# Three pieces of K and V per head instead of four blocks, and x read as one row, in a decode attention kernel that reads 282 MB

## The chip, the cores and the metric

One core of a Trainium2 chip. The metric is the device time of one execution in microseconds (us), median over several. The "span" is the profiled time from the first to the last instruction; it is usually some 1.4 us shorter than the time. PE is the matrix engine, DVE the vector engine, ACT the scalar engine, SP the engine whose queue issues the loads. A load "lands" when its completion is signalled; its "forerunner" is the load ahead of it in the queue, and its "lead" is how long before the forerunner's landing it is issued. Where a run fell in the slow state it is left out and named.

## The reference

One new token (batch 1) attends over a cache of 65,536 positions in 8 key/value heads, four query heads on each, followed by a small gated MLP. Everything is bf16.

```python
B, Sq, D = 1, 1, 512
Hq, Hkv, Sk, Dh = 32, 8, 65536, 128            # k_cache, v_cache: (1, 8, 65536, 128)
def _A_ref(x, k_cache, v_cache, wq, wo):
    q = (x @ wq) ...                           # 32 heads of 128
    k, v = repeat(k_cache, 4), repeat(v_cache, 4)
    scores = einsum("bhqd,bhkd->bhqk", q, k) * Dh ** -0.5
    p = softmax(scores)
    return einsum("bhqk,bhkd->bhqd", p, v) ... @ wo
x = A_x
h = x + _A_ref(layernorm(x), A_k_cache, A_v_cache, A_wq, A_wo)
g, u = layernorm(h) @ w_gate, layernorm(h) @ w_up      # 512 -> 1792
return h + (sigmoid(g) * u) @ w_down                   # 1792 -> 512
```

K and V are 134.2 MB each and are used once. The rest (w_q, w_o, the MLP) is 14 MB.

## The kernel before

K and V lie in SBUF in a ring of four slots, one slot for a block of 16,384 positions: 128 rows of 32 KB, 4 MiB. One queue (SP) issues every load in a fixed order; each load waits until what stood in its slot has been used. A head is four K blocks and four V blocks, alternating, with V one head behind K.

```python
order = [("wq", 0)]
order += [("K", b) for b in range(NR)]                       # NR = 4 blocks a head
for b in range(NR, NB):                                      # NB = 32
    order += [("K", b), ("V", b - NR)]
order += [("V", NB - 4), ..., ("V", NB - 1), ("wg", 0), ("wu", 0), ("wd", 0)]
...                                                          # slot_of, prev: who frees the slot
dma("act", lambda e: e.dma_start(x_col[:, :], A_x[0].rearrange("o (p k) -> (o p) k", k=4)), "x", name="x")
V_SPLIT = [(0, 3), (3, 4)]                                   # the very last V block comes in two pieces
...
    src = cache[0, h, r * BLK:(r + 1) * BLK, :].rearrange("(p t) d -> p (t d)", t=T)     # 128 rows of 32 KB
    dma("sp", lambda e, d=dst, sr=src: e.dma_start(d, sr), ..., deps, f"{k}{b}")
if ld == ("V", NB - 4):
    ...                                                      # w_o, after the first V block of the last head
```

```python
label("values", "part")
e.reg_mov(m, NR); e.reg_mov(k, 0); e.reg_mov(v, v_even)
...                                       # V0..V3: waits for the block, by branches once per block
goto("sums", "values")
pv_regs(e)                                # 14 register additions: the addresses of the round
goto("products", "sums")
section("B")                              # the eight matmuls
e.reg_alu(p, p, 2 * 512, ALU.add)
e.reg_alu(v, v, 2 * 2 * CH, ALU.add)
e.reg_alu(m, m, -1, ALU.add)
e.br_ne(m, 0, on_true="sums", on_false="sums_end")
```

After the last V piece come w_o's second part, a layernorm, w_gate and w_up, the gate, and w_down: 56 small matmuls, four at a time, whose weights are the last bytes to land.

Of the kernel before, what the change touches and what calls it, by code (L numbers as in the profile page):

```python
# [35 lines left out]
class Prog:  # L36
# [26 lines left out]
    def emit(self):  # L63
# [3 lines left out]
        needed = {d for ops in self.ops.values() for o in ops for d in o["deps"]} | set(self.at_end)  # L67
# [20 lines left out]
        for e, ops in self.ops.items():  # L88
            n = 0
            for o in ops:  # L90
                if o["dma"]:
                    k, v = o["dma"]
                    value[o["name"]] = (self.dma_sems[k]["sem"], v, k)
                elif o["to"]:
                    k = o["to"]
                    counts[k] = counts.get(k, 0) + 1
                    if o["name"]:
                        value[o["name"]] = (extra[k], counts[k], k)
                    o["inc"] = True
                elif o["name"] in needed or o.get("inc"):  # L100
                    n += o["times"]
                    value[o["name"] or id(o)] = (sems[e], n, e)
                    o["inc"] = True
# [110 lines left out]
def bass_sequential_preLN__gqa_block_cached__glu_gated_glu__decode_kernel(  # L214
# [10 lines left out]
    SLOT = T * DH  # L225
    CH = TC * DH
    NF = FF // 128
# [6 lines left out]
    with ExitStack() as es:  # L234
# [16 lines left out]
        ring = sb("ring", [128, NSLOT * SLOT], bf16)  # L251
# [9 lines left out]
        x_col = sb("x_col", [128, 4], bf16)  # L261
# [40 lines left out]
        def slot_ap(s):  # L302
            return ring[:, s * SLOT:(s + 1) * SLOT]

# [4 lines left out]
        order = [("wq", 0)]  # L309
        order += [("K", b) for b in range(NR)]  # L310
        for b in range(NR, NB):
            order += [("K", b), ("V", b - NR)]
        order += [("V", NB - 4), ("V", NB - 3), ("V", NB - 2), ("V", NB - 1), ("wg", 0), ("wu", 0), ("wd", 0)]
        slot_of, prev = {}, {}
        for i, ld in enumerate(order):
            if ld[0] == "V" and ld[1] >= NB - NR:
                slot_of[ld] = slot_of["V", ld[1] - 2]
                prev[ld] = ("V", ld[1] - 2)
            elif ld[0][0] == "w" and i:
                slot_of[ld] = 3 if ld[0] == "wd" else 1  # L320
                prev[ld] = ("K", NB - 1 if ld[0] == "wd" else NB - 2)
            else:
                slot_of[ld] = i % NSLOT
                prev[ld] = order[i - NSLOT] if i >= NSLOT else None

        def freed(ld):
            if ld is None:
                return None
            k, b = ld
            return {"wq": "q", "K": f"F{b}", "V": f"PV{b}"}[k]  # L330

        dma("act", lambda e: e.dma_start(x_col[:, :], A_x[0].rearrange("o (p k) -> (o p) k", k=4)), "x", name="x")
        V_SPLIT = [(0, 3), (3, 4)]
        W_SPLIT = {"wg": [(0, 4)], "wu": [(0, 3), (3, 4)]}
        W_AT = {"wg": 0, "wu": 4 * FF}
        for ld in order:
            k, b = ld
            s = slot_of[ld]
            dst = slot_ap(s)
            deps = [freed(prev[ld])]  # L340
            if k == "wq":
                dma("sp", lambda e, d=dst: e.dma_start(d.rearrange("p (k n) -> p k n", k=4),
                    A_wq.rearrange("(p k) n -> p k n", p=128)), f"r{s}", deps, "wq")
            elif k in ("wg", "wu"):
                w = B_w_gate if k == "wg" else B_w_up
                dst, src = dst[:, W_AT[k]:W_AT[k] + 4 * FF], w.rearrange("(p k) n -> p (k n)", p=128)
                for i, (k0, k1) in enumerate(W_SPLIT[k]):
                    dma("sp", lambda e, d=dst, w=src, a=k0 * FF, z=k1 * FF: e.dma_start(d[:, a:z], w[:, a:z]),
                        f"{k}{i}", deps if i == 0 else (), f"{k}.{i}")
            elif k == "wd":  # L350
                src = B_w_down.rearrange("(p r) n -> p r n", p=128)
                for i, (r0, r1) in enumerate(WD_SPLIT):
                    dma("sp", lambda e, d2=dst[:, r0 * D:r1 * D].rearrange("p (r n) -> p r n", n=D), sr=src[:, r0:r1, :]:
                        e.dma_start(d2, sr), f"wd{i}", deps if i == 0 else (), f"wd{i}")
            else:
                h, r = b // NR, b % NR
                cache = A_k_cache if k == "K" else A_v_cache
                src = cache[0, h, r * BLK:(r + 1) * BLK, :].rearrange("(p t) d -> p (t d)", t=T)
                if ld == ("V", NB - 1):
                    for i, (c0, c1) in enumerate(V_SPLIT):  # L360
                        d2, s2 = (ap[:, 2 * c0 * CH:2 * c1 * CH] for ap in (dst, src))
                        dma("sp", lambda e, d2=d2, s2=s2: e.dma_start(d2, s2),
                            "v0" if i else "vl", deps if i == 0 else (), f"V{b}.{i}")
                else:
                    dma("sp", lambda e, d=dst, sr=src: e.dma_start(d, sr), f"v{s}" if k == "V" else f"k{s}" if k == "K" and b >= NR else f"r{s}",
                        deps, f"{k}{b}")
            if ld == ("V", NB - 4):
                for i, (j0, nj) in enumerate(WO):
                    src = A_wo[j0 * DH:(j0 + nj) * DH, :].rearrange("(p r) n -> p (r n)", r=nj)
                    dst = ktw[:, j0 * D:(j0 + nj) * D]  # L370
                    dma("sp", lambda e, src=src, dst=dst: e.dma_start(dst, src), f"wo{i}",
                        [f"G{HKV - 1}"] if i == 0 else (), f"wo{i}")
# [44 lines left out]
        ln_stats(0, lambda e: e.tensor_copy(hT[0][:, :], x_col[:, :]), "x", 0, 0)  # L417
# [36 lines left out]
        def project_q(e):  # L454

            e.reg_mov(reg(e, 0), addr_of(xz, 8 + 7))
            e.reg_mov(reg(e, 4), addr_of(ring, slot_of[("wq", 0)] * SLOT))
# [3 lines left out]
            with e.Fori(0, HKV):  # L461
                for kt in range(4):
                    mm_at(e, ps(1, 0, 512, 0, 8), at_reg(xz, reg(e, kt), [[4 * 16, 128], [1, 8]]),
                          at_reg(ring, reg(e, 4 + kt), [[NSLOT * SLOT, 128], [1, 512]]), False, 32)
# [36 lines left out]
        def dve_block(b):  # L501
            s = slot_of[("K", b)]
            for c in range(NC):
                n = b * NC + c
                at = s * SLOT + (2 * (c % NR) + c // NR) * CH
                src = ring[:, at:at + CH].bitcast(fp32)
                dst = ktw[:, (n % NKT) * CH:(n % NKT + 1) * CH].bitcast(fp32)
                deps = [f"K{b}"] if c == 0 else []
                if b % NR or b == 0:
                    deps.append(f"S{b - 1}.{c}" if b else None)  # L510
                op("dve", lambda e, d=dst, sr=src: e.transpose(d, sr), deps, f"T{b}.{c}", to="T")  # L511
            op("dve", lambda e: e.memset(scr[:, b:b + 1], 0.0), (), f"F{b}")
# [49 lines left out]
        def transposed(h):  # L562

            for b in range(NR * h, NR * h + NR):
                op("dve", lambda e, b=b: e.transpose(PT_sb[:, (b % 4) * 512:(b % 4 + 1) * 512],  # L565
                                                     P_sb[:, (b % 4) * 512:(b % 4 + 1) * 512]),
                   [f"E{b}", f"oxq{h - 1}" if h else None], f"PT{b}", to="PT" if b % NR == NR - 1 else None)
# [7 lines left out]
        def pv_regs(e):  # L575
            for half in range(NC // NR):
                for tq in range(4):
                    i = 8 * half + tq
                    if i:
                        e.reg_alu(reg(e, i), R["p"], 2 * (128 * tq + half), ALU.add)  # L580
                        e.reg_alu(reg(e, i + 4), R["v"], 2 * (half * TC + 4 * tq) * 128, ALU.add)

        def pv(b):
            h, r = b // NR, b % NR
            if r == NR - 1:
                P.part["pe"] = ("VL", b)
                op("pe", lambda e: None, [f"V{b}" if b < NB - 1 else f"V{b}.1"])
            P.part["pe"] = ("B", b)
            for half in range(NC // NR):
                for tq in range(4):  # L590
                    i = half * 8 + tq
# [3 lines left out]
                        at_reg(ring, reg(e, i + 4) if i else R["v"], [[NSLOT * SLOT, 128], [1, 512]]), False, 32, 32 * tq),  # L595
                       (), f"PV{b}" if half and tq == 3 else None, times=NR)

        def head_out(h):
            op("act", lambda e: e.activation(po_sb[:, :], ps(PO, 0, 512), AF.Copy, scale=rl[:, :]),  # L599
               [f"PV{NR * h + NR - 1}", f"rl{h}"], f"po{h}", to="po")  # L600
            for t in range(4):
                op("pe", lambda e, t=t: e.matmul(ps(OX, 0, 4), lhsT=po_sb[:, t * 128:(t + 1) * 128],  # L602
                                                 rhs=sel_bf[:, 8 * t:8 * t + 8:2], start=(t == 0), stop=(t == 3)),
                   [f"po{h}"] if t == 0 else (), f"ox{h}" if t == 3 else f"oxq{h}" if t == 2 else None,
                   to="Q" if t == 2 else None)
# [30 lines left out]
        def project7():  # L636
            regroup(0)
            waits = ["O3.0", "wo0"]
            def rows(e):
                out = ps(YB, 0, D, 0, 1)  # L640
                e.matmul(out, lhsT=O3[:, 0:1], rhs=ktw[:, 0:D], start=True, stop=False, skip_group_check=True)
                ra, ro, rb, rp, left = (reg(e, i) for i in range(5))
# [26 lines left out]
        def pe_flow(e, section):  # L669
# [7 lines left out]
            i, w, p, v, m, k = (R.setdefault(n, e.alloc_register(f"r_{n}")) for n in "iwpvmk")  # L677
            w0, p0 = addr_of(ktw, W0 + NC - 1 + 127), addr_of(PT_sb, 31 * 4)
            v_even, v_odd = (addr_of(ring, slot_of[("V", b)] * SLOT) for b in (0, 1))
            e.reg_mov(i, 0)  # L680
            goto("head")
            e.reg_mov(w, w0)
            e.reg_mov(p, p0)
            goto("part")
            e.br_eq(i, HKV, on_true="last", on_false="scores")
# [9 lines left out]
            away("br_eq", w, w0 - 12, "maxima", lambda: section("X"))  # L695
            e.br_eq(i, 0, on_true="next", on_false="values")
            label("values", "part")
            e.reg_mov(m, NR)
            e.reg_mov(k, 0)
            e.reg_mov(v, v_even)  # L700

            def odd_late():
                e.reg_mov(v, v_odd)
# [168 lines left out]
```

## Time and profile before

| | before |
|---|---|
| time, median of the first 3 runs | 658.38 us (658.36 to 658.48) |
| span of the profiled run | 657.1 us |
| busy share: DMA queue / PE / DVE / ACT | 99.7% / 64% / 53% / 7% |
| x landed / projection of the query ended | 14.8 / 27.7 us |
| last V piece landed / last PV matmul ended | 641.98 / 644.21 us |
| last weights landed / the matmuls that need them start | 654.83 / 654.87 us |

The main lines of the page stand in the prediction below. A line of the timeline reads: start, duration, engine, source line, operation, destination<-sources, count, and in brackets the idle time just before and what ended it.

From the view that cuts the run into stretches, for the last 1.90 us of matrix work (columns: stretch and length, busy time and count of PE, weight loads, DVE, ACT, POOL, then PE's granted clock, the DMA share and GB/s):

```profile
653.40:655.30 1.90, 1.68 (x56) 1.26 (x56) 0.13 (x1) 0.00 (x0) 0.00 (x0) 0.50 0.50 196
```

The DMA still works in this stretch: in the kernel before, w_down's last third comes in while PE is in the earlier ones.

### The profile page before, as it was taken

Reading aid. Unit: us, or ns where it says so; the run is one execution under the profiler, and the core shown is the slowest. Engines: PE = TensorE matmul, PEld = TensorE weight load, DVE = VectorE, ACT = ScalarE, POOL = GpSimd, SP = SyncE. Lnnn points to the kernel's source line nnn. Section 1 sums busy time; section 2 is a strip of 40 time slices with the busy share of each in tenths; the row PEclk is TensorE's granted clock in tenths of the full one; section 3 lists DMA queues with packets and bytes.
Section 4 is the critical chain, followed back from the end, with each engine's and each line's share of the span. In section 5 each row is a group of like instructions: output and inputs, shape, how many; then the busy total and the mean of one; then the engine's idle time right before and its main releaser. Section 6 shows DMA issues by size and latency. Waiting matters only on the chain. (4 is left out here: it accounts for less than half of the span.)

```text
span 657.1 us, 6111 instructions
## 1 busy us (share of the span) xinstructions
PE 420.5 (64%) x2315; PEld 74.1 (11%) x1547; DVE 349.7 (53%) x439; ACT 42.9 (7%) x114; POOL 3.6 (1%) x17
## 2 busy tenths in 40 slices
PE   0688488548666585576765575764866668556746
PEld 0200011011000010010100110101100001001322
DVE  2399775547537665347555374465743575542202
ACT  1100200020000200020000200002000100002001
POOL 1000000000000000000000000000000000000000
PEclk9989689677888697776966769765888869677676
DMA  9999999999999999999999999999999999999998
GB/s 383 447 433 429 439 423 431 431 447 415 447 415 447 437 425 447 415 447 419 443 441 421 447 415 447 423 439 443 419 447 415 447 427 435 445 417 427 435 430 352
DMA packets 10802, 282.34 MB, mean 430 GB/s; under 512 B 1329, under 2 KB 1330, under 8 KB 1842
## 3 DMA queue, kind: packets, MB, share of 16 engines
q1 hardware_dynamic: 10658, 282.33, 99.7%
q10 hardware_dynamic: 144, 0.00, 0.0%
HBM read 282.33 MB, written 0.00 MB: 430 GB/s over the span
## 5 line engine op out<-in xcount | busy, mean ns | idle before, releaser
L431 PE MATMUL PS<-ktw 128*128 128x512 bf16 x1024 | 299.9, 442 | 157.4 <-DVE ktw L511 153.6
L511 DVE STREAM_TRANSPOSE ktw<-ring 128x1024 f32<-128x1024 f32 x256 | 291.6, 1205 | 128.0 <-DMA ring<-in_A_k_cache_dram 128.0
L431 PE MATMUL PS<-ring,PT_sb 128*32 x1024 | 83.9, 455 | 23.6 <-issue 13.2
L431 PEld LDWEIGHTS PS<-ktw 128*128 x256 | 27.1, 106 | 408.2 <-issue 256.8
L565 DVE STREAM_TRANSPOSE PT_sb<-P_sb 128x512 bf16<-128x512 bf16 x32 | 20.2, 684 | 54.0 <-PE PS L602 52.3
L551 ACT ACTIVATE negmax<-PS 128x1 f32<-128x1 f32 x8 | 1.4, 171 | 520.6 <-PE PS L549 520.6
L431 PEld LDWEIGHTS PS<-ring,PT_sb 128*32 x1024 | 25.8, 116 | 79.8 <-issue 74.6
L516 DVE TENSOR_REDUCE M_sb<-PS 128x1 f32<-128x512 f32 x32 | 19.9, 684 | 25.5 <-PE PS L431 25.5
L555 ACT ACTIVATE P_sb<-PS,negmax 128x512 bf16<-128x512 f32 x32 | 21.6, 686 | 0.3
L572 DVE TENSOR_REDUCE lsum<-PS 128x1 f32<-128x4 f32 x8 | 1.3, 163 | 31.2 <-PE PS L570 31.2
L542 PE MATMUL PS<-identf,gm 128*1 128x128 f32 x16 | 3.4, 301 | 16.9 <-DVE gm L540 16.9
L616 DVE TENSOR_TENSOR Lw<-O,blk_of 128x896 bf16<-128x896 bf16 (+1 forms) x2 | 1.4, 683 | 20.6 <-ACT O L606 20.6
L402 PE MATMUL PS<-st,onesf 128*128 128x2 f32 x4 | 1.2, 362 | 16.1 <-DVE st L401 16.1
L431 PE MATMUL PS<-ring,xz 128*8 x32 | 9.2, 459 | 2.3 <-issue 2.3
L599 ACT ACTIVATE po_sb<-PS,rl 128x512 bf16<-128x512 f32 x8 | 5.5, 687 | 53.2 <-PE PS L431 53.2
L431 PE MATMUL PS<-ktw,O 128*1 x26 | 7.6, 464 | 0.0
L549 PE MATMUL PS<-one_f,gmrep 1*128 1x1 f32 x16 | 4.2, 330 | 5.0 <-DVE gmrep L546 5.0
L555 ACT ACTIVATION_READ_ACCUMULATOR P_sb<-PS,negmax 128x1 f32 x32 | 6.5, 202 | 0.0
L476 DVE STREAM_TRANSPOSE qt<-qh 32x512 bf16<-32x512 bf16 x1 | 0.7, 699 | 10.6 <-ACT qh L473 10.6
L602 PE MATMUL PS<-sel_bf,po_sb 128*128 128x4 bf16 x32 | 2.0, 168 | 6.4 <-ACT po_sb L599 6.4
L417 DVE CAST hT<-x_col 128x4 f32<-128x4 bf16 x1 | 0.2, 171 | 10.6 <-DMA x_col<-in_A_x_dram 10.6
L661 DVE COPY yr<-PS 1x512 f32<-1x512 f32 x1 | 0.7, 679 | 8.3 <-PE PS L659 8.3
(82 smaller groups left out, 74.0 us busy)
## 6 DMA issues: line engine op xcount, KB each, us to landing
ring<-in_A_k_cache_dram SPq DMA_DIRECT2D x32, 4096.0 KB, 28.7
ring<-in_A_v_cache_dram SPq DMA_DIRECT2D x31, 4096.0 KB, 26.4
ring<-in_A_wq_dram SPq DMA_DIRECT2D x1, 4096.0 KB, 12.3
ktw<-in_A_wo_dram SPq DMA_DIRECT2D x1, 3584.0 KB, 12.7
ring<-in_A_v_cache_dram SPq DMA_DIRECT2D x1, 3072.0 KB, 13.2
ring<-in_B_w_gate_dram SPq DMA_DIRECT2D x1, 1792.0 KB, 19.0
ring<-in_B_w_up_dram SPq DMA_DIRECT2D x1, 1344.0 KB, 21.7
ring<-in_A_v_cache_dram SPq DMA_DIRECT2D x1, 1024.0 KB, 15.2
```

The source lines that it names most:

```text
L431: return e.add_instruction(mybir.InstMatmult(name=nc.get_next_instruction_name(), engine=mybir.EngineType.PE, ins=[rhs, lhsT], outs=[e.low ...
L511: op("dve", lambda e, d=dst, sr=src: e.transpose(d, sr), deps, f"T{b}.{c}", to="T")
L516: op("dve", lambda e, u=u: e.tensor_reduce(M_sb[:, u % 4:u % 4 + 1], ps(u % NS, 0, 512), AX.X, ALU.max), [f"S{b}.{NC - NR + k}"], f"mx{u}" ...
L542: op("pe", lambda e: e.matmul(ps(MISC, 0, 128, 0, 1), lhsT=gm[:, :], rhs=identf[:, :], start=True, stop=True), [f"gm{h}"], f"gmT{h}", to="Q")
L549: op("pe", lambda e: e.matmul(ps(MISC, 128, 129), lhsT=gmrep[0:1, :], rhs=one_f[0:1, 0:1], start=True, stop=True), [f"gmrep{h}"], f"neg{h}")
L551: op("act", lambda e: e.activation(negmax[:, k:k + 1], ps(MISC, 128, 129), AF.Copy, scale=-att_scale), [f"neg{h}"], f"negmax{h}")
L555: op("act", lambda e, b=b: e.activation(P_sb[:, (b % 4) * 512:(b % 4 + 1) * 512], ps(b % NS, 0, 512), AF.Exp, bias=negmax[:, k:k + 1], sca ...
L565: op("dve", lambda e, b=b: e.transpose(PT_sb[:, (b % 4) * 512:(b % 4 + 1) * 512], P_sb[:, (b % 4) * 512:(b % 4 + 1) * 512]), [f"E{b}", f"o ...
L572: op("dve", lambda e: e.tensor_reduce(lsum[:, :], ps(MISC, 132, 136), AX.X, ALU.add), [f"l{h}"], f"ls{h}", to="D")
L599: op("act", lambda e: e.activation(po_sb[:, :], ps(PO, 0, 512), AF.Copy, scale=rl[:, :]), [f"PV{NR * h + NR - 1}", f"rl{h}"], f"po{h}", to ...
L602: op("pe", lambda e, t=t: e.matmul(ps(OX, 0, 4), lhsT=po_sb[:, t * 128:(t + 1) * 128], rhs=sel_bf[:, 8 * t:8 * t + 8:2], start=(t == 0), s ...
L616: op("dve", lambda e: e.tensor_tensor(Lw[i][:, :].rearrange("p (j c) -> p j c", j=n), bass.AP(tensor=O2, offset=j0, ap=[[NQ, 128], [1, n], ...
```

## The change

Its intent: fewer and longer transfers, so that less is lost between them. A head's K and V come in three pieces of 48, 32 and 48 KB a row (12, 8 and 12 chunks) instead of four of 32 KB; rows of the cache are assigned to partitions by piece. The ring keeps its size, but its places now overlap between heads, so the order of loads and what frees them are written out. w_o is issued between the first two V pieces of the last head. x is read as one row of 1 KB and turned into four columns by four matmuls. On PE, the wait for a piece can now fall in the middle of a loop of ten rounds, so the round itself tests whether it has come to a wait. The diff also moves work that has nothing to do with the loads: DVE transposes a head's probabilities only after the first eight chunks of the next head, and the matmuls that turn w_o's row into columns (2.0 us at 638.08 before) come ahead of the last head's second piece.

```diff
-        x_col = sb("x_col", [128, 4], bf16)
+        x_row = sb("x_row", [1, D], bf16)
...
+    PIECES = ((0, 12), (12, 20), (20, 32))
+    AT = {"K": (0, 0, 8), "V": (12, 24, 20), "K0": (0, 12, 20), "V7": (0, 12, 20), "wq": 24, "wg": 0, "wd": 7}
...
+        dma("act", lambda e: e.dma_start(x_row[:, :], A_x[0]), "x", name="x")
+        LAST = [(20, 28), (28, 32)]
...
+            rows = cache[0, h, j0 * TC * 128:j1 * TC * 128, :].rearrange("(p t) d -> p (t d)", p=128)
...
+        for h in range(1, HKV):
+            load("K", h, 0, ["F0.1" if h == 1 else f"F{h - 1}.3"], "ka", f"K{h}.0")
+            load("V", h - 1, 0, ["F0.3" if h == 1 else f"PV{h - 2}.3:2"], "va", f"V{h - 1}.0")
+            load("V", h - 1, 1, ["F0.4" if h == 1 else f"PV{h - 2}.3"], "vb", f"V{h - 1}.1")
+            load("K", h, 1, [f"F{h}.0"], "ka", f"K{h}.1")
+            load("K", h, 2, [f"F{h}.1", f"PV{h - 1}.0:4"], "kb", f"K{h}.2")
+            load("V", h - 1, 2, [f"PV{h - 1}.0"], "vb", f"V{h - 1}.2")
+        h = HKV - 1
+        load("V", h, 0, [f"F{h}.3"], "va", f"V{h}.0")
...                                                   # w_o here, after PV{h - 1}.3
+        load("V", h, 1, (), "vm", f"V{h}.1")
+        for i, cols in enumerate(LAST):
+            load("V", h, 2, (), ("vb", "vl")[i], f"V{h}.2{('', 'b')[i]}", cols)
...
+        for k in range(4):
+            op("pe", lambda e, k=k: e.matmul(ps(0, 4 + k, 5 + k), lhsT=bass.AP(tensor=x_row, offset=k, ap=[[D, 1], [4, 128]]),
+                                             rhs=sel_bf[0:1, 0:1], start=True, stop=True, skip_group_check=True),
...
             goto("sums", "values")
             pv_regs(e)
+            def waits():
+                e.reg_alu(c, c, 8, ALU.add)
+                e.br_eq(w, w0, on_true="second", on_false="fourth")
+                ...                                   # the second piece, w_o's rows
+                label("fourth", "waits")
+                e.br_ne(i, i_last, on_true="products", on_false="last_rounds")
+                label("last_rounds", "fourth")
+                section("VL")                         # wait for the very last piece
+            away("br_eq", p, c, "waits", waits, "products")
             goto("products", "sums")
             section("B")
-            e.reg_alu(p, p, 2 * 512, ALU.add)
+            e.reg_alu(p, p, s, ALU.add)
+            e.reg_alu(s, s, step[0] ^ step[1], ALU.bitwise_xor)
             e.reg_alu(v, v, 2 * 2 * CH, ALU.add)
             e.reg_alu(m, m, -1, ALU.add)
```

## The prediction

No term of the forecast's sum is among them: the sum came to 0.73 + 0.05 = 0.78 us, and so to 657.6 us. The rate of 435.2 GB/s in it (its "ceiling", from which also the 99.5%, the 77.10 us, the 51.20 us and the 648.75 us come) was not yet shown by the trace of before, whose packets give 435.0. It stands because the packets of both traces give it: 8192 B are recorded as 309 ns (medians), and in the trace of after 49152 B as 1815, so 40960 B in 1506 ns, times 16 engines 435.2 GB/s. One nanosecond in the 1506 moves the 9.638 us by 6 ns, so the 46 ns per transfer are an estimate, and an experiment below gives about 40. The start-up "of about 2 us" is an estimate from the trace of before too, where the first packet starts 1.03 us after the first issue.

> **What bounds the kernel now.** I read the page from the transfers upward: HBM bytes and DMA share first, then whether the share ever drops, then what the end hangs on.

> ```profile
> span 657.1 us, 6111 instructions
> DMA  9999999999999999999999999999999999999998
> q1 hardware_dynamic: 10658, 282.33, 99.7%
> q10 hardware_dynamic: 144, 0.00, 0.0%
> HBM read 282.33 MB, written 0.00 MB: 430 GB/s over the span
> ```

> The DMA engines are busy in every slice, 99.7% of the span. PE is busy 64% and DVE 53%, so the compute engines have room. q10 is the read of x: 128 rows of 8 bytes each and 16 completions, 144 packets for 1 KB. The transfers view gives the lead with which loads are issued and the landing times:

> ```profile
> ring<-in_A_k_cache_dram SPq DMA_DIRECT2D x32, 4096.0 KB, 28.7
> ring<-in_A_v_cache_dram SPq DMA_DIRECT2D x31, 4096.0 KB, 26.4
> ring<-in_A_wq_dram SPq DMA_DIRECT2D x1, 4096.0 KB, 12.3
> x_col<-in_A_x_dram ACTq DMA_DIRECT2D x1, 1.0 KB, 14.0
> ```

> A 4 MiB load lands 28.7 us (median) after its issue although one takes under 10 us: two others stand ahead of it. The queue's own waits (over 19 us at the longest, for DVE to free K or PE to free V) are therefore hidden. The pace is best read from the waits of DVE for K, in the timeline of DVE; these two lines are six heads apart:

> ```profile
> 99.62 9.13 DVE L511 STREAM_TRANSPOSE ktw<-ring 128x1024 f32<-128x1024 f32 x8 [1.33 <-DMA ring<-in_A_k_cache_dram]
> ...
> 564.43 9.13 DVE L511 STREAM_TRANSPOSE ktw<-ring 128x1024 f32<-128x1024 f32 x8 [9.48 <-DMA ring<-in_A_k_cache_dram]
> ```

> (564.43 - 99.62) / 6 = 77.468 us per head of eight 4 MiB transfers: 9.684 us each, 433.1 GB/s, with no room for a bubble of even a microsecond. The landing records say the same: 9.67 to 9.71 us between any two neighbours from 12.3 us on.

> The end, from the timeline: the last V pieces, then the short MLP while its weights still come in.

> ```profile
> 640.17 2.72 PE L431 MATMUL PS<-ring,PT_sb 128*32 x24
> 643.26 0.91 PE L431 MATMUL PS<-ring,PT_sb 128*32 x8 [0.37 <-PEq L169]
> 648.72 3.15 PE L813 MATMUL PS<-ring,hc 128*1 128x448 bf16 x32 [0.25 <-DVE hc L800]
> 653.58 1.68 PE L831 MATMUL PS<-ring,hhT 128*1 128x128 bf16 x56 [0.98 <-DVE hhT L826]
> 655.96 0.33 SPq L841 DMA_DIRECT2D out_dram<-y_sb  x1
> ```

> The third w_down piece lands at 654.83 us (issued at 629.6, 25.2 us to landing), and its eight matmuls start at 654.87. PE had begun the ones before at 654.72, one group per 0.107 us, so without the wait it would have gone on at about 654.83. Transfers and the PE chain arrive together: the end moves earlier only if both do. After it come the y copies and the store, 2.2 us to the end of the span.

> [...] a packet of 32768 B is recorded as 1213 ns and one of 8192 B as 309 ns; the slope, 24576 B in 904 ns, times 16 engines is 435.0 GB/s. The kernel runs at 99.5% of that. [...] the 8-byte packets of x run from 5.4 to 14.4 us, eight per engine, about one per 1.2 us, which is one 32 KB packet of wq or K. [...]

> **The change part by part.**

> *Fewer, larger loads.* The bytes stay. At 435.2 GB/s 4 MiB take 9.638 us; they take 9.684, so a queued transfer costs 46 ns beyond its bytes: eight data packets and one completion per engine, 5 ns each. The tail confirms that this hardly depends on size: from the landing of V at 603.13 to the last weights at 654.83, 12 transfers of 0.26 to 4 MB bring 22.28 MB in 51.70 us; the bytes take 51.20; 0.50 / 12 = 42 ns. A piece of 48 KB a row still has 128 rows, so eight packets per engine, so again some 46 ns. Counts: before, 32 K + 33 V + 1 wq + 2 wo + 6 MLP = 74. After, 24 K + 25 V (the last piece cut in two) + 9 = 58. Saved: 16 x 0.046 = 0.73 us, all on the path that sets the end. Per head: six transfers instead of eight, 77.10 + 6 x 0.046 = 77.38 us.

> *x as a row.* 128 packets fewer. The first K intervals, in which they ran, are 9.70 and 9.71 us against 9.684: 0.04 to 0.05 us saved. x lands at some 6 to 7 us instead of 14.8, and four one-column matmuls (about 0.5 us) are added; from landing to ready query took 14.80 to 18.28 = 3.5 us, so PE could start at about 11, and then waits for wq at 12.3. The projection (9.4 us) ends near 22 instead of 27.7: 6 us earlier. Its worth at the end is zero, because the queue is full at that time: it only releases the third piece of K0 earlier.

> *Hand-offs.* Each load must be issued before its forerunner has landed, less a start-up of about 2 us (first issue at 0, first bytes between 1 and 2 us). The smallest lead in the old trace, w_o's issue at 598.92 against a landing at 603.13, is 4.2 us and left no visible gap. New order in a head: K0, V0, V1, K1, K2, V2 of 14.5, 14.5, 9.7, 9.7, 14.5, 14.5 us. With t = 0 at the start of K0: K2 lands at 62.9, DVE needs four transposes of 1.14 us, so the next K0 is issued at 67.7, due at 77.4: lead 9.7. K1 (free after eight chunks of K0, about 24; due 38.7) 14. K2 (four PV rounds of 0.9 us after V0 has landed at 29, about 33; due 48.4) 15. V2 (all ten rounds, 43; due 62.9) 20. The next V0 (two of the last six rounds, about 82; due 91.9) 10. At the first head, where softmax lies between, K1 of head 1: its forerunner lands at 89.7, head 0's softmax ends near 72, eight transposes to 82: about 7. w_o after the first V7 piece: PV of head 6 ends near 602, due 608: 6. All above 4.2, so no stall is expected.

> *The end.* After the last V piece (16 KB a row instead of 8) two rounds of eight matmuls remain instead of one: 0.9 us more. But the old chain did not hang on that landing (641.98, used from 643.26, when the three rounds and the branch before it were over; PV done at 644.21 = landing + 2.23). In the new kernel the four rounds on the bigger piece (lands 4.9 us earlier) are over first; then 0.25 us to start and 1.85 us for two rounds: landing + 2.1. The four fp32 column matmuls (2.0 us at 638.08, just ahead of the old last rounds) move into the idle time before. So chain and weights shift alike.

> Sum: 0.73 + 0.05 = 0.78 us; 658.38 - 0.78 = 657.6 us.

> **The rivals.**

> 1. *The start counts.* Six microseconds earlier query, so about 652. For it: PE's wait before the projection and the late x. Against: DMA 9 in the first slices, and K landing every 9.7 us all through the projection.
> 2. *The larger pieces stall the queue.* Three pieces give coarser releases, and PE now waits for V1 in the middle of a part. A lead that shrinks to nothing costs its shortfall once per head: 1 us each would give 664 or so. Against: the leads above, and compute at half load.
> 3. *Long rows are cut into more packets.* Nothing before is longer than 32768 B. If 48 KB became two packets at 5 ns each, 32 pieces with eight extra per engine cost 1.3 us, more than is saved: 658.9.
> 4. *The PE chain takes the end.* If the two rounds, or fetching their branch code, come out 0.9 us longer than counted, nothing is left of the gain, since the chain has no slack to the weights: 658.5.

> **Range and chances.** Rivals 3 and 4 put the upper end near 658.7; a somewhat larger saving per transfer, or a shorter tail, the lower at 656.8. The old bytes alone take 648.75 us at the ceiling, and start-up (2.6 us before steady flow) and end (2.3 us after the last landing, 1.3 us from span to time) stay, so even with no per-transfer cost at all it would be some 655: faster by over 2% (645.2) is shut out by the bytes. Slower by 2% (671.6) needs rival 2 on a large scale. 0.005, 0.985, 0.01.

> **What would show it right or wrong.** DMA queue: near 8450 packets (58 x 144 and the store) if 48 KB is one packet. DVE's waits for K: 77.38 us per head. x: landing below 8 us, projection from about 12.5. Last weights at about 654.05. A 7 or 8 in the DMA row, or K waits further apart than 77.5, would mean rival 2; about 12500 packets rival 3; last weights early but the end unmoved, rival 4. A first-slice gain that survives to the end would refute my claim that x is hidden.

## More of the kernel before

The "granted clock" is the share of its full speed at which PE is let run.

Before, PE's timeline at the last head's third block:

```profile
632.81 3.61 PE L431 MATMUL PS<-ring,PT_sb 128*32 x32 [6.47 <-PEq L169]
```

Thirty-two matmuls are four rounds; their first matmuls start at 632.81, 633.64, 634.49 and 635.35, so a round takes 0.85 us.

## The result, and the profile after

| | before | after |
|---|---|---|
| time, median of 6 runs each | 658.46 us (658.36 to 658.98) | 657.96 us (657.40 to 658.45) |
| ratio, with 95% interval | | 0.9991 (0.9978 to 1.0004): the same |
| span of the profiled run | 657.1 us | 657.1 us |
| last V piece landed / last PV matmul ended | 641.98 / 644.21 us | 640.91 / 644.33 us |
| last weights landed | 654.83 us | 653.75 us |

A ratio here is the mean time of one kernel's fast runs over the mean of the other's of the same rounds, so it is not quite the ratio of the medians quoted. Lines of the page after:

```profile
DMA  9999999999999999999999999999999999999997
...
q1 hardware_dynamic: 8354, 282.33, 99.5%
q10 hardware_dynamic: 2, 0.00, 0.0%
```

8354 packets are 58 transfers of 144 and two for the store: a row of 48 KB is one packet (recorded as 1815 ns; 32 KB took 1213). q10, the read of x, went from 144 packets to 2. No slice but the last shows a digit below 9; that one fell from 8 to 7, because the transfers end earlier in it. In DVE's timeline, the waits for K six heads apart:

```profile
99.30 9.13 DVE L500 STREAM_TRANSPOSE ktw<-ring 128x1024 f32<-128x1024 f32 x8 [9.94 <-DMA ring<-in_A_k_cache_dram]
...
563.49 9.13 DVE L500 STREAM_TRANSPOSE ktw<-ring 128x1024 f32<-128x1024 f32 x8 [16.25 <-DMA ring<-in_A_k_cache_dram]
```

(563.49 - 99.30) / 6 = 77.365 us per head, against 77.468 before. At the start, PE's timeline:

```profile
7.00 0.29 PE L402 MATMUL PS<-sel_bf,x_row 1*128 1x1 bf16 x4 [7.00 <-DMA x_row<-in_A_x_dram]
...
12.87 9.81 PE L419 MATMUL PS<-ring,xz 128*8 x32 [4.35 <-DMA ring<-in_A_wq_dram]
```

x is there at 7.0 instead of 14.8, and the projection now waits for w_q and is over at 22.7 instead of 27.7. So far this is the prediction. The end is not quite; PE's timeline there, and the store:

```profile
636.67 4.47 PE L419 MATMUL PS<-ring,PT_sb 128*32 x32 [3.70 <-PEq L171]
642.15 2.17 PE L419 MATMUL PS<-ring,PT_sb 128*32 x16 [1.01 <-issue]
...
653.47 1.66 PE L823 MATMUL PS<-ring,hhT 128*1 128x128 bf16 x56 [0.97 <-DVE hhT L818]
...
655.82 0.33 SPq L833 DMA_DIRECT2D out_dram<-y_sb  x1
```

The four rounds on the bigger part of the last block take 4.47 us where four took 3.61; they start at 636.67, 637.82, 638.98 and 640.09, 1.11 to 1.16 us apart. The granted clock does not explain this: it was 0.50 in both stretches. At that clock rounds written out without registers start 0.84 to 0.85 us apart (in an experiment below), just as the old ones do, so the old round was as long as its matmuls; its sequencer's work was some 0.76 us (two rounds at a clock of 1.00, from 624.2 us on in the trace of before) and lay hidden behind them. The new round is as long at either clock. These are the last two rounds of the run with the pieces alone (below), the first of them at a clock of 1.00:

```profile
642.30 0.63 PE L415 MATMUL PS<-ring,PT_sb 128*32 x8 [1.43 <-issue]
643.41 1.01 PE L415 MATMUL PS<-ring,PT_sb 128*32 x8 [0.48 <-issue]
```

Eight matmuls are over in 0.63 us, and the next eight still start 1.11 us after the first: in the new loop the sequencer sets the pace.

The store is only 0.14 us earlier than before (655.82 against 655.96). The chain of what ended last shows the same stretch step by step (start, duration, what):

```profile
640.09 1.05 PE PS L419 x6
641.14 1.01 issue
642.15 1.05 PE PS L419 x8
643.20 0.06 issue
```

The last V piece landed at 640.91, but its first round starts at 642.15: 1.24 us later, of which 1.01 us lies between two rounds in which PE's sequencer was busy with nothing that the profile names ("issue"); between the other rounds it is 0.06 to 0.11. PV ends at 644.33, 0.12 us later than before, although the piece came 1.07 us earlier. PE reaches w_down at 653.47, when the last weights are about to land (653.75, 0.28 us later), and then works through the 56 matmuls without a wait. **The end has moved from the weights to the PE chain.**

With that the end depends on the clock that PE is granted in its last two microseconds. The same kernel profiled again, and the same stretch in both (first the run above, then the second):

```profile
653.40:655.30 1.90, 1.66 (x56) 1.37 (x56) 0.13 (x2) 0.12 (x1) 0.00 (x0) 0.50 0.00 0
```

```profile
653.40:655.30 1.90, 0.95 (x56) 0.77 (x56) 0.56 (x2) 0.54 (x2) 0.00 (x0) 1.00 0.00 0
```

At a clock of 0.50 the matmuls take 1.66 us, at 1.00 they take 0.95; the spans of the two runs are 657.1 and 656.3. The DMA share is 0 in both, where it was 0.50 before. The six spans of the changed kernel (657.1, 657.0, 656.9, 656.3, 656.0, 656.0) fall into two groups 0.6 to 1.1 us apart, as this would make them; the mean granted clock of a whole run (0.774 to 0.786) does not tell the groups apart, and only profiled runs show the clock of the last stretch.

### The profile page after: what moved, and what is told of

It reads as the page before. It is cut to its first block, busy times and chain, and to the rows that moved or that the text cites. A ratio compares the mean times of both kernels' runs of the same rounds, so it can differ in the third digit from the quotient of the medians.

```text
span 657.1 us, 6298 instructions
## 1 busy us (share of the span) xinstructions
PE 441.4 (67%) x2319; PEld 70.5 (11%) x1551; DVE 350.4 (53%) x432; ACT 42.9 (7%) x114; POOL 3.6 (1%) x17
## 2 busy tenths in 40 slices
DMA packets 8356, 282.33 MB, mean 430 GB/s; under 512 B 930, under 2 KB 932, under 8 KB 1444
## 3 DMA queue, kind: packets, MB, share of 16 engines
q1 hardware_dynamic: 8354, 282.33, 99.5%
HBM read 282.33 MB, written 0.00 MB: 430 GB/s over the span
## 5 line engine op out<-in xcount | busy, mean ns | idle before, releaser
L419 PE MATMUL PS<-ktw 128*128 128x512 bf16 x1024 | 294.9, 440 | 109.9 <-DVE ktw L500 103.2
L419 PE MATMUL PS<-ring,PT_sb 128*32 x1024 | 105.4, 506 | 66.5 <-PEq L171 34.9
L419 PEld LDWEIGHTS PS<-ring,PT_sb 128*32 x1024 | 21.8, 116 | 145.3 <-issue 143.6
L507 DVE TENSOR_REDUCE M_sb<-PS 128x1 f32<-128x512 f32 x32 | 19.9, 684 | 19.5 <-PE PS L419 19.5
L535 DVE TENSOR_REDUCE gmj<-PS 1x4 f32<-1x128 f32 x8 | 2.2, 279 | 44.6 <-PE PS L533 44.6
L561 PE MATMUL PS<-L_sb,lsel 128*128 128x4 f32 x16 | 2.5, 229 | 3.8 <-DVE PT_sb L556 3.8
## 6 DMA issues: line engine op xcount, KB each, us to landing
ring<-in_A_v_cache_dram SPq DMA_DIRECT2D x9, 4096.0 KB, 30.1
ring<-in_A_k_cache_dram SPq DMA_DIRECT2D x8, 4096.0 KB, 24.7
ring<-in_A_wq_dram SPq DMA_DIRECT2D x1, 4096.0 KB, 12.2
ktw<-in_A_wo_dram SPq DMA_DIRECT2D x1, 3584.0 KB, 14.4
```

What stands on the lines that cost most here:

```text
L419: return e.add_instruction(mybir.InstMatmult(name=nc.get_next_instruction_name(), engine=mybir.EngineType.PE, ins=[rhs, lhsT], outs=[e.low ...
L507: op("dve", lambda e, u=u: e.tensor_reduce(M_sb[:, u % 4:u % 4 + 1], ps(u % NS, 0, 512), AX.X, ALU.max), [f"S{b}.{NC - NR + k}"], f"mx{u}" ...
L535: op("dve", lambda e: e.tensor_reduce(gmj[:, :], ps(MISC, 0, 128, 0, 1).rearrange("p (i a c) -> p a i c", a=4, c=NC), AX.XY, ALU.max), [f" ...
L561: op("pe", lambda e: e.matmul(ps(MISC, 132, 136), lhsT=lsel[:, :], rhs=L_sb[:, :], start=True, stop=True), [f"PT{NR * h + NR - 1}"], f"l{h ...
```

## The experiments

Three theories were set against each other.

- **A.** Fewer transfers save their fixed cost all along, the row of x next to nothing, and what arrives earlier at the end is partly lost because the new loop makes the rounds longer, so that the PE chain holds the end.
- **B.** The end is still on the transfers, and the longer rounds are harmless.
- **C.** The gain, as far as there is any, comes from the start (x).

### The changed kernel again, twice

> The changed kernel once more, beside the others on one chip. Theory A (the transfers got about 1 us shorter, but the PE chain after the last V piece got longer and now sets the end): last weights land near 653.8 us, the last w_down matmuls start well after that, and the time is 0 to 0.6 us below the kernel before. Rival B (the end hangs on the weights as it did before, and the small gain seen is scatter between chips): time 0.8 to 1.1 us below the kernel before.

> The changed kernel for comparison on this chip: spans from 655.9 to 657.1, the low ones in runs in which the clock granted at the end is high; last weights near 653.75 in all.

No edit. Measured: medians 657.99 and 657.95 us, ratios 0.9990 (0.9977 to 1.0003) and 0.9990 (0.9976 to 1.0004). With the first result these are three sets on different occasions whose means lie 0.62, 0.67 and 0.61 us below those of before. (The medians differ by 0.50, 0.58 and 0.31.) Each interval just includes 1; that all three means agree makes a gain of some 0.6 us likely, if far below 2%, but does not show it. The last weights land at 653.72 and 653.70 (653.75 in the first profile): the landing times repeat to 0.05 us. The spans (means 656.50 and 656.46, before 656.98 and 656.84) put the gain at 0.4 to 0.5 us. Why time and span differ by 0.2 us is not known.

### The pieces alone, and the row alone

```diff
# the pieces alone: the changed kernel with x as columns
-        x_row = sb("x_row", [1, D], bf16)
+        x_col = sb("x_col", [128, 4], bf16)
-        dma("act", lambda e: e.dma_start(x_row[:, :], A_x[0]), "x", name="x")
+        dma("act", lambda e: e.dma_start(x_col[:, :], A_x[0].rearrange("o (p k) -> (o p) k", k=4)), "x", name="x")
...
# the row alone: the kernel before with these lines the other way round
```

> The changed kernel with the old read of x (128 rows of 8 bytes). Theory A: w_q and all later loads land 0.05 to 0.1 us later than in the changed kernel, x lands near 14 us, the projection ends near 28 us and the third piece of K0 is still issued before the queue is empty; time within 0.15 us of the changed kernel. Rival (the start counts): 2 us or more slower than the changed kernel.

> The kernel before, with only x read as one row and turned by four matmuls. Theory A: x lands near 6.7 us instead of 14.8, the query is ready 5 us earlier, w_q and all later loads land 0.05 to 0.1 us earlier, the time falls by 0.05 to 0.15 us and no more, as the queue is full while the query is made. Rival (the start counts): 2 to 6 us faster.

PE's timeline at the projection with the pieces alone (with the row alone it starts at 12.83):

```profile
19.48 8.44 PE L415 MATMUL PS<-ring,xz 128*8 x32 [2.31 <-issue]
```

With the pieces alone the projection is 6.6 us later than in the changed kernel, yet every landing differs from it by no more than 0.05 to 0.13 us, and the last weights land at 653.85: 0.98 us earlier than before. Theory C falls. With the row alone they land at 654.41, 0.42 us earlier than before. The two parts do not add up to the 1.08 us of both, and the reason lies mostly in the one trace of before: against each of four other builds of it (the row alone, and three runs below, of which two also have a slower pace of their own) its landings fall back once by some 0.25 us between 61 and 119 us. What this slip is, isn't known. Without it the pieces alone save 0.73, the row alone 0.17 and both 0.83 us. The start of a run (w_q landed between 12.14 and 12.54 us in the profiles) also shifts everything after it, so the share of x, 0.1 to 0.2 us, can't be fixed more closely from single traces. In time, the pieces alone took 658.53 us (ratio 1.0000, 0.9986 to 1.0013).

The row alone took 661.61 us (ratio 1.0038, 1.0021 to 1.0055), which no theory had expected. The loss is not within the program as profiled: the spans average 656.80 against 656.98 before, but in five of six runs the time exceeds the span by 4.7 to 5.3 us instead of some 1.4. What happens in those three microseconds, and why with this build, stays open (its trace shows a packet of instructions just after the end, but so does that of before: 16 KB, 1.22 us, 1.3 us after the span). It says nothing against the row in the changed kernel, whose times exceed its spans by the usual amount.

### What a transfer costs: more packets, more transfers

The prediction put the whole gain on 46 ns per transfer. Two experiments on the kernel before separate packets from transfers. In the first each row of a K or V block is two runs of 16 KB (twice the data packets, the same 74 transfers); in the second each block is loaded by two transfers (twice the packets and twice the transfers).

```diff
# two runs
+                    src = src.rearrange("(a p t) d -> p a (t d)", a=2, p=128)
+                    dst = dst.rearrange("p (a x) -> p a x", a=2)
# two transfers
-                    dma("sp", lambda e, d=dst, sr=src: e.dma_start(d, sr), ...)
+                    for y in range(2):
+                        dma("sp", lambda e, d=dst, sr=src, y=y: e.dma_start(d[:, y * 4 * CH:(y + 1) * 4 * CH], sr[:, y * 4 * CH:(y + 1) * 4 * CH]), ...)
```

> The kernel before, with each row of K and V (but the last block's) made of two runs of 16 KB from two places: same bytes, same 74 transfers, 16 data packets per engine and transfer instead of 8. Which token a row holds changes for K and V alike, so the result stays. If the 46 ns per transfer belong to its packets (5 ns each): 62 x 8 x 5 = 2.5 us later. If they belong to the transfer: no change.

> The kernel before, with every K and V load cut into two transfers of half the row: 138 transfers instead of 74, packets of 16 KB as in the run with two runs a row. Either way 64 x 46 ns = 2.9 us later in the last landing; what it has over the run with two runs a row is the cost of a transfer beside its packets: about 0.4 us if packets carry the cost, all of 2.9 if the transfer does.

DVE's waits for K six heads apart, first with two runs, then with two transfers:

```profile
99.82 9.13 DVE L516 STREAM_TRANSPOSE ktw<-ring 128x1024 f32<-128x1024 f32 x8 [2.87 <-DMA ring<-in_A_k_cache_dram]
...
566.33 9.13 DVE L516 STREAM_TRANSPOSE ktw<-ring 128x1024 f32<-128x1024 f32 x8 [9.33 <-DMA ring<-in_A_k_cache_dram]
```

```profile
100.01 9.13 DVE L514 STREAM_TRANSPOSE ktw<-ring 128x1024 f32<-128x1024 f32 x8 [2.20 <-DMA ring<-in_A_k_cache_dram]
...
567.06 9.13 DVE L514 STREAM_TRANSPOSE ktw<-ring 128x1024 f32<-128x1024 f32 x8 [8.96 <-DMA ring<-in_A_k_cache_dram]
```

Two runs: 466.51 / 6 = 77.752 us per head, 0.284 more than before for eight transfers, 35.5 ns each, or 4.4 ns for each of the eight extra packets on an engine. Two transfers: 467.05 / 6 = 77.842, 0.374 more, 46.8 ns for each extra transfer. But that trace has a disturbance of its own: a packet of 8 KB of instructions at 354.00 us, 0.31 us long (the row "q14 instruction: 1, 0.01, 0.0%" of its page), and the first landing after it (362.93) is 0.43 us later than the others lead one to expect. In the landings from 178 to 353 us and from 373 to 567 us, on either side of it, an extra transfer costs 40 to 41 ns, and in the run with two runs eight extra packets cost 38 ns. So what a transfer costs beyond its packets is some 3 ns, not the 11 that the two lines suggest. The last weights land 2.09 and 2.94 us later than before, and the times are 660.69 (ratio 1.0043, 1.0029 to 1.0056) and 661.25 us (1.0042, 1.0028 to 1.0056). Of the prediction's 46 ns some 40 are confirmed, and nearly all of them are the packets: one longer row in place of two shorter ones is what pays, the number of transfers itself pays little.

### w_o ahead of the last head's first V piece

```diff
-        load("V", h, 0, [f"F{h}.3"], "va", f"V{h}.0")
         for i, (j0, nj) in enumerate(WO):
             ...
+        load("V", h, 0, [f"F{h}.3"], "va", f"V{h}.0")
```

> The changed kernel with w_o ahead of the first V piece of the last head instead of behind it. Its buffer is free only when the last PV of head 6 is done, near 601 us, while the load ahead of it has landed near 592: theory: the queue stands empty from 592 to about 603 and the time rises by 9 to 12 us. Rival (the place of w_o does not matter, the queue has lead enough): within 0.5 us of the changed kernel.

Measured, in two runs: 677.98 us (ratio 1.0297, 1.0278 to 1.0315), 20 us longer than the changed kernel. The page's DMA row, then PE's timeline:

```profile
DMA  9999999999999999999999999999999999949992
```

```profile
629.57 6.54 PE L419 MATMUL PS<-ring,PT_sb 128*32 x48 [20.63 <-PEq L171]
```

w_o is issued at 601.25, when PV of the head before is over, but its forerunner had landed at 592.6: the queue is empty, and w_o lands at 612.51, 19.9 us after its forerunner instead of 8.5. That is the expected bubble of 11.4 us (the last weights land 11.6 us later). The other 8 us I had not expected: PE gets the first V piece late, then has all rounds and w_o's rows still before it, and its last rounds end 11.6 us after the last V piece has landed. So the place that the change gives w_o is no detail; in it, w_o is issued 5.9 us ahead of its forerunner's landing, and nothing is lost.

### The last six rounds written out

If the longer rounds hold the end (A), rounds without registers should bring PV's end to some 2 us after the landing, and the weights should hold the end again. Here the six rounds of the last head's third piece are 48 matmuls with fixed addresses.

```diff
+            def last_values():
+                section("VX0")          # four rounds, 32 matmuls
+                section("VL")           # wait for the very last piece
+                section("VX1")          # two rounds, 16 matmuls
+            away("br_eq", i, i_last, "last_values", last_values, "sums_end")
```

> The changed kernel, with the last head's last six PV rounds written out as 48 matmuls without the loop, its register work and its branches; loads and order as in the changed kernel. Theory A: PV of the last head ends about 2.1 us after the last V piece has landed instead of 3.45, so the chain reaches w_down before its last piece, whose landing stays near 653.75; the end moves back onto the weights: 0.8 to 1.0 us below the changed kernel of the same rounds, span about 656.2. Rival B: the weights set the end already, no change against the changed kernel (within 0.2).

Measured: 658.80 us (ratio 1.0002, 0.9989 to 1.0015), 0.8 us slower than the changed kernel of the same rounds (spans 657.0 to 657.6 against 655.9 to 657.0), where a gain was expected. A row of the page's queues that the changed kernel does not have (packets, MB, share), then PE's timeline:

```profile
q8 instruction: 1, 0.02, 0.0%
```

```profile
642.16 1.90 PE L419 MATMUL PS<-ring,PT_sb 128*32 128x512 bf16 x16 [0.82 <-DMA ring<-in_A_v_cache_dram]
...
653.28 2.13 PE L843 MATMUL PS<-ring,hhT 128*1 128x128 bf16 x56 [1.03 <-DVE hhT L838]
```

On PE's side the expectation held: the last rounds start 0.04 us after the landing (642.12) instead of 1.24, PV ends at landing + 1.9, and the last eight w_down matmuls start at 655.03, just after their weights (654.99). But the weights themselves are 1.2 us late, and so is everything from 99 us on: in DVE's timeline the wait for K that was at 99.30 is at 100.62, and the one at 563.49 at 564.69.

```profile
100.62 9.13 DVE L500 STREAM_TRANSPOSE ktw<-ring 128x1024 f32<-128x1024 f32 x8 [10.95 <-DMA ring<-in_A_k_cache_dram]
...
564.69 9.13 DVE L500 STREAM_TRANSPOSE ktw<-ring 128x1024 f32<-128x1024 f32 x8 [14.98 <-DMA ring<-in_A_k_cache_dram]
```

Up to there landings agree with the changed kernel. Just before, at 93.9 us, lies the one packet of the new row "q8 instruction" on the page: 16 KB of instructions, 0.92 us. That they are PE's is inferred: this build differs from the changed kernel in PE's code alone. The delay of 1.2 to 1.3 us is carried to the end. Why it is not made up for is not shown: the trace does not say which DMA engine the packet was on. That a queue which is 99.5% busy has no idle time to catch up in is my reading.

### Only the last two rounds written out, behind the loop

To keep the code shorter, only the two rounds after the last landing are written out; once on the changed kernel, once with x as columns.

```diff
+            def last_rounds():
+                section("VL")
+                section("VX1")
+            def outs():
+                away("br_eq", i, i_last, "last_rounds", last_rounds)
+                section("O")
+            away("br_eq", w, w0 - 12, "outs", outs)
```

> The changed kernel, with only the last head's last two PV rounds written out, behind the code of the loop instead of within it (the run with all six written out had its transfers held up 1.3 us from 99 us on[...]). Theory A: last V piece lands near 640.9, PV ends about 2.1 us later instead of 3.45, the last weights land near 653.75 and set the end again: span 656.0 to 656.3 in every run whatever the clock, where the changed kernel has 655.9 to 657.1. Time 0.7 to 1.0 us below the kernel before. Rival B (the weights set the end already): span of the slow-clock runs of the changed kernel, 657.0. If a 16 KB read falls among the transfers again, the weights come up to 1.3 us later and the end with them.

> The same with the old read of x, which leaves out four matmuls: less code on PE, in case the 16 KB read comes with the length of the code. Theory A: as before but all landings 0.1 us later, span 656.1 to 656.4. Rival B: 657.0.

Measured: 658.76 us (ratio 1.0004, 0.9991 to 1.0018) and 659.25 us (1.0010, 0.9997 to 1.0024): slower than the changed kernel again (spans 657.3 to 657.5 and 657.3 to 657.9 against 656.1 to 657.1). PE's timeline of the first:

```profile
641.35 1.65 PE L419 MATMUL PS<-ring,PT_sb 128*32 128x512 bf16 x16 [0.16 <-issue]
...
649.72 1.66 PE L821 MATMUL PS<-ring,hc 128*1 128x448 bf16 x16 [0.72 <-DMA ring<-in_B_w_up_dram]
...
653.32 2.10 PE L839 MATMUL PS<-ring,hhT 128*1 128x128 bf16 x56 [1.22 <-DMA ring<-in_B_w_down_dram]
```

The last V piece lands at 640.93, within 0.02 us of the changed kernel, and PV ends at landing + 2.1, as the prediction had it for the change. Then a packet of 16 KB of instructions comes at 644.6 (0.94 us), w_gate lands 1.46 us later than in the changed kernel and the last weights at 655.00, 1.25 us later; PE waits for w_up and for w_down. The second has the packet at 644.81 and the last weights at 655.23. So where the code packet lies, in the middle of the run or near its end, the transfers after it are late, by 1.2 to 1.5 us for a packet of 0.92 to 0.94 us, and those before it are not. The 8 KB packet of the run with two transfers shows the same on a smaller scale (some 0.4 us for 0.31).

The size of PE's code goes with it. The builds without such a 16 KB packet before the last weights have 30,208 to 31,680 bytes of it as compiled (before 31,104, the changed kernel 30,784), the three with one have 32,448, 33,024 and 36,928. I did not isolate the size from the layout of the branches, so this is a correlation over the builds. (The 8 KB packet above stands in another row, q14, and in a build of 31,104 bytes; why it came is not known.) (Some of the shorter builds, the kernel before among them, show the packet after the last weights have landed, where it can delay no load.)

### Two counted loops

If written-out code costs a read of code, the loop can be made shorter instead: the wait is taken out of the round, which then has one test less, by counting the rounds before and after it.

```diff
+                e.reg_alu(m, c, 0, ALU.add)      # the rounds after the wait
+                e.reg_mov(c, 0)
 ...
-            away("br_eq", p, c, "waits", waits, "products")
             goto("products", "sums")
 ...
             label("sums_end")
+            away("br_ne", c, 0, "waits", waits, "sums")
```

> The changed kernel, with its PV rounds in two counted loops and the waits for the next piece between them, instead of a test in every round and a detour of three branches before the last two; no matmul written out, so the PE code stays as short as in the kernel before (31104 bytes; the versions with matmuls written out had 32448 to 36928, the changed kernel 30784). Theory A: no 16 KB read among the transfers, last V piece at 640.9 and last weights at 653.75 as in the changed kernel; a round takes about 1.0 us instead of 1.11 and the detour about 0.6 us more than a normal round's step instead of 1.0; PV ends 2.4 to 2.7 us after the last piece instead of 3.45; spans 656.0 to 656.4 with less scatter than the changed kernel's 655.9 to 657.1; time 0.6 to 1.0 us below the kernel before. Rival B (something else than the chain holds the end): spans as those of the changed kernel.

```profile
636.85 3.99 PE L419 MATMUL PS<-ring,PT_sb 128*32 x32 [5.53 <-PEq L171]
641.86 2.08 PE L419 MATMUL PS<-ring,PT_sb 128*32 x16 [1.01 <-DMA ring<-in_A_v_cache_dram]
...
653.15 1.66 PE L828 MATMUL PS<-ring,hhT 128*1 128x128 bf16 x56 [0.97 <-DVE hhT L823]
```

No code packet. A round takes 0.98 us (four in 3.99 instead of 4.47), the last rounds start 0.64 us after the landing at 641.22 instead of 1.24, and PV's end comes at landing + 2.7. PE reaches w_down 0.32 us before the changed kernel did, although in this profile all landings are 0.31 us later (from w_q on, so from the start of the run, not from the edit). The mean of the five spans (656.7, 655.9, 656.0, 656.0, 656.6) is the lowest of any build: 656.24, against 656.89 for before in the same rounds. The time is 658.01 us (657.29 to 658.40), ratio 0.9987 (0.9973 to 1.0001; one slow run of before is left out). The mean is 0.68 us below that of before, the changed kernel's 0.6 to 0.67: no difference between the two is shown. That PE gets to the end sooner is shown, that the time gets shorter by it is not.

### A longer round in the kernel before

The reverse test: the loop of the kernel before gets a branch that is never taken and two register operations that change nothing.

```diff
             pv_regs(e)
+            away("br_eq", p, 1, "nowhere", lambda: None)
 ...
             e.reg_alu(p, p, 2 * 512, ALU.add)
+            e.reg_alu(p, p, zero, ALU.add)
+            e.reg_alu(p, p, zero, ALU.bitwise_xor)
```

> The kernel before, with one never-taken compare-and-branch and two register operations added to each PV round; no load changed. Theory A (a PV round is as long as its sequencer work, and the chain sets the end as soon as it is longer than the weights' way): a round of eight matmuls takes about 1.1 us instead of 0.9, the last weights land at 654.8 as before, the end is 0.6 to 0.9 us later. Rival B (the weights set the end): no change within 0.2 us.

Measured: 661.48 us (ratio 1.0047, 1.0034 to 1.0060); a round takes 1.13 to 1.18 us instead of 0.85 (0.76 for the old sequencer's work alone). That three such instructions make the loop this much longer is shown. But the time does not separate A from B, because the weights did not stay where they were: they land 2.4 us later. The last V block is loaded into a place that an earlier block must leave first; with longer rounds that is 5.8 us later (632.16 instead of 626.38), and its issue comes 0.2 us after its forerunner has landed (631.96). Its first part then takes 9.99 us from landing to landing instead of 7.32: a bubble of 2.7 us. A slower loop on PE, an engine 64% busy before, cost most of the time through the hand-off of a buffer. The trace does show A's part as well: PE reaches w_down at 657.22, 3.64 us later than before, where the weights came only 2.41 us later (657.24), and runs through the 56 matmuls without a wait.

## Why the prediction was right, and where it was not

- **The total and the class:** right. 657.6 was predicted; the medians are 657.95 to 657.99, in the range. The range (656.8 to 658.7) also holds the 658.46 of before, so the total alone tells little about the mechanism.
- **Packets:** 48 KB is one packet, rival 3 is out. "Near 8450" was my arithmetic: 58 x 144 is 8352, and 8354 were counted.
- **The pace:** 77.38 us per head predicted, 77.365 measured. The mechanism (a small fixed cost per transfer on a queue that is never empty) is confirmed by the two experiments that raise it; its size is rather 40 than 46 ns, and the packets make nearly all of it. (77.468 for before contains some 0.1 us of the slip in six heads; without it the gain is 0.086 us a head, 43 ns for each transfer saved.)
- **The saving in the transfers:** 0.78 us predicted, 1.08 in the profile (last weights), of which some 0.25 are the slip in the trace of before: 0.83 remain.
- **x:** hidden, as said; rival 1 is out. Six microseconds at the start are worth 0.1 us in the landings of the comparison with the pieces alone. But the 0.04 to 0.05 us that the prediction read from two intervals of 9.70 and 9.71 us were not to be read there: the landings of 4 MiB loads in that trace do not come 9.67 to 9.71 us apart, as it says, but 9.62 to 9.76 all through. (The 8-byte packets of x, too, end at 13.2 us; those up to 14.4 are its completions.)
- **Hand-offs:** no bubble, rival 2 is out. The predicted leads were w_o 6, the second K piece of head 1 7, the next K 9.7, the first V 10, the third K piece 15, the third V piece 20 us; measured 5.9, 9.7, 9.8, 11.2, 13.6 and 19 to 20. The two experiments that let a lead fall below zero (-8.6 and -0.2 us) had bubbles of 11.4 and 2.7 us, 2.8 and 2.5 us more than the lead that was missing.
- **The end: the step that failed.** "0.25 us to start and 1.85 us for two rounds: landing + 2.1" came out as 1.24 and 2.18: landing + 3.4. I took some 0.9 us for a round from the old loop, whose length was that of its matmuls at half clock, and did not count what the diff adds to the sequencer's work: one test and one register operation in each round, and a way over three branches to the wait. So this work, 0.76 us a round before and hidden, became 1.11 to 1.17 us and visible. The four rounds that were to be over before the last piece landed ended 0.23 us after it (641.14), and the way to the wait took another 1.01 us, where 0.25 in all was counted for the start. Rival 4 had named it with a threshold ("0.9 us longer than counted") and it was 1.3 longer. "Chain and weights shift alike" is therefore wrong: the weights moved by 1.08 us and the chain's arrival at w_down by 0.11 (653.58 to 653.47).
- **Why the total is right all the same:** what remains of the gain depends on the clock at the end. Before, the weights came last in the profile (landed at 654.83, used from 654.87), and a faster PE could, by this reading, do little with it; now the chain is last, and with a clock of 1.00 the 56 matmuls are over 0.71 us sooner. In profiles with the half clock the span is that of before (657.1), with the full clock it is 0.8 less. The average over runs, 0.4 to 0.5 us in spans and 0.6 in times, is smaller than predicted and came about otherwise than predicted; that the total is only 0.3 to 0.4 us off is in part luck: how much of the gain the longer chain takes back depends on the clock of the last stretch, which the prediction did not consider.

What isn't shown: that the two groups of spans are the two clocks in the runs without a profile; where the 1.01 us of the way to the wait go exactly; that a shorter chain alone shortens the time (the three builds that shortened it most were held by later weights, and the fourth differs by less than the noise); what the slip in the trace of before is; what lies in the three microseconds outside the span with the row alone.

## What to carry to other kernels

On this queue, 99.5 to 99.7% busy, fewer and longer rows saved a few nanoseconds per packet (4.4 to 4.7 ns on an engine), and the sum could be predicted from the trace to within some tenths of a microsecond (0.78 us predicted, 0.83 measured without the slip); but the end moves only as far as the compute chain behind it lets it (the weights came 1.08 us earlier, the chain reached w_down 0.11 us earlier), so the sequencer's work that a change adds to a loop (tests, registers, the way to a wait; here a round went from 0.85 to 1.11 us and more, and the way to the wait took 1.01) belongs in the sum with its own duration. Before writing code out to save that work, look whether a read of instructions appears in the profile: here, on a queue 99.5% busy, the delay of 1.2 to 1.3 us that came with one packet of 0.92 us stayed to the end. And the lead of each issue over its forerunner's landing told beforehand which orders of loads were free (5.9 us and more) and which cost a bubble (-8.6 us, 11.4 us of it).
